# Threshold attention and maxout FFN on one core: another written order of the same work, with another list of masked score pieces

## The chip, the cores and the metric

The kernel runs on one core of one Trainium2 chip. The metric is device time in microseconds (us) from start to end of one execution. The kernel before took 447.18 us, the median of 3 runs (446.42 to 448.04).

## The reference

```
scores = scale * q @ k.T                     # batch 8, 8 heads, 576 x 576, head size 64
thresh = max(scores, axis=-1) - tau          # tau = 0.02
scores = where(scores >= thresh, scores, -1e9)
attn   = exp(scores - max(scores)); attn = attn / (sum(attn) + 1e-9)
x      = (attn @ v), heads side by side      # 4608 tokens x 512
h      = max(max(x @ w1, x @ w2), x @ w3)    # 768 wide
out    = h @ w_out                           # 4608 x 512
```

The softmax thus keeps only those scores of a row that lie within tau of the row's largest.

## The kernel before, in words

The attention of a batch is done in two quads of four heads, 16 quads in all. A quad is cut into nine chunks of 128 query rows, a chunk into two halves r of one head each; this gives 288 **score pieces** (a half chunk, 128 rows by 576 scores). A piece goes through this line, one letter for each step:

- `S` (`scores`, line 280, TensorE): the fp32 score matmuls into one of four PSUM slots; the digit behind the letter is the slot.
- `m` (`maximum`, line 312, VectorE, DVE): the row maximum, read out of the slot.
- `e` (`exponents`, line 324, ScalarE, ACT): the exponential, or the step that flattens the values below the threshold.
- `k` or `n` (`numerators`, line 332): the numerators and their sum, `k` on DVE, `n` on ACT.
- `r` (`reciprocals`, DVE), `p` (`normalized`, line 344, GpSimd, POOL) and `t` (`turned`, line 353, a transposing DMA issued by SP), the last for both halves together.

There are two ways through this line, and the string `MASKED` (line 24) chooses one for each piece, a bit each:

```
        if masked(c["g"], c["idx"], r):     # maximum: copies the scores out of PSUM
            vector.tensor_scalar(out=z_of(c, r), in0=c[r], scalar1=-1.0, ... accum_out=nm)
...
        if masked(...):                     # exponents: one ACT step, on the copy
            scalar.activation(out=zn, in_=zn, func=AF.Exp, bias=c["bias", r], scale=-1.0)
        else:                               # reads PSUM
            scalar.activation(out=zn, in_=c[r], func=AF.Prelu, ..., alpha=FLAT)
...
        if masked(...):                     # numerators, letter k
            vector.scalar_tensor_tensor(out=zn, in0=zn, scalar=thr, ... accum_out=acc)
        else:                               # letter n
            scalar.activation(out=zn, in_=zn, func=AF.Exp, scale=-1.0 / FLAT, accum_out=acc)
```

A **masked** piece costs DVE two passes (m, k) and ACT one (e), and its slot is free when m has read it. A **flat** piece costs DVE one pass (m) and ACT two (e, n), and its slot is free when e has read it.

The other letters: `T` transposes q or k of the next quad (evacuated by `a` on ACT for q and `c` on DVE for k, and copied across partitions by `q` on POOL); `O` multiplies numerators and values (evacuated by `x` on ACT or `w` on DVE); `F` is the first half of an FFN piece and `B` the second half of the oldest one begun, for the hidden layer (evacuated by `h` on ACT, `v` on DVE) and for the output projection (`u` on ACT, store `o` on SP). `l` and `g` are loads on SP, `y` and `z` casts on POOL. `S`, `T`, `O` and `F` each take one of the four slots.

The string `ORDER` (line 39) is the whole program after the prologue, one letter after the other; the loop at line 666 issues them. `_Ordered` (line 81) ties every instruction to the one before on the same engine, so each engine, SP included, works its letters off strictly in the written order, and across engines only the data and the buffers bind: a slot can be written again when its reader is done, `z` has four buffers for each half (`ZBUFS`), `P` six (`PBUFS`).

The last batch is split into two parts (`SPLIT`), so that the FFN of its first part fills TensorE while the attention of its second part ends.

Of the kernel before, what the change touches and what calls it, by code (L numbers as in the profile page):

```python
# [21 lines left out]
FLAT = 2.0 ** -100  # L22

MASKED = """
001100101001000000011101001010000001100010001000101000011000100000100000
000011111001100001001001001001000001011100101001000110001010010000010011
000010011101100001001100100001001010001100010111000001000100000110000101
001001001101100000110001000100100100001100100011100111010011010111110110
"""


# [5 lines left out]
PBUFS = 6  # L37

ORDER = """
lllS0llmlS1yelgS2ymylS3emgnlT0mleS1lakS2nlqermS3ylmeS0pmeS1kpS3elmS2nlzmelrmnT1pS0tcnperkT1pameS1zmteS3knpS0  # L40
rnmpemS2permeqS1mnqT3meqktepS0ncS2ntrpmS3npretprmeS1pmnS0tpmS3npmS1etpmeS0rT2mnplkeT1akgeS2qmgepmteS3rkpeknt
S0perrnmT2pncS3ptamepS1meqtrS2meyqnS3lmqeS0pmelpknT1lpS2nmeymeS3lrkepS0tcnT2rpnmS1tpnmaprrmS0eS2pmteS1pmT3ep
ctepmeT3O0ykntnyS2etrykpnO1wnprmaS0xptrS3meS2zmeS1mzgeS0mlnS3pmleS1pmelO2qmelpkteO0nrnklpS3nlwgxprrmS2leS0pm
eF3qtmT1eBqcF0eqkthBpnS2vS1nF3pmnF0pmBerBkepS2vhT1tnprmS0S3apmetS1zmeS2rmpeF3tmF0epBkepF1tnBvBznvS2ghS3rymnF
0gmS1eplBrkepF2tnmF3BnpvBnqvT1S0hprrcT2S3pamS1eymzF2emBeqgkF0etyS3nS1vpnmtF2pBmezBveS3prgnS0mtS1phrmT3epO2me
tzeF0wpnS1gcqS2nmBqnmO3zekepgS1xvlF2nS3mtnF0rrmpBeBlpveS1lphS2mntF3zmeBrpS0evS1lpnmF2lnpS3rmleBptmS1nzvS0nS3
mtpnS2rpeF1rmepmtepS0mBepmtekF3ektekT2uBarklpukS0uqlS2urS1mlnS3pmleO0pmlepmelO2wtnkS1xrS0tepmF2myF3eBkepT1tB
hcF0nqvT2T1laByrcynS3qvS2nlqmF1tnpF0meS3pBelmBlhrrF2kpelS1vnBlprF3mnlS0pveBtprmS1hS2pmeS3tpmeS0pmF2emF1eBkeT
3BvatF0nvqT2T3BkqlaS1nrcS3phmtS2npmF0epF1mteBqkBeqF3lnvS2lnBrvplS0hmtpS1F3meS2mteBrmepS0vnpO1rekpnO3mtnpweS2
yrrtxS1mF0yymT3epBcnS1pvS2nptF3meS0pmeBomT2hS1okeF0omF3ntBkaBervS1ponrF2vpemS0ptuS3mpeF2metknT1T3rknBparrceS  # L50
0puS3mqtuS1mpeS2mpeS3lmF0peomepS1ketqT3S2ncBqnmlqnmlO3ekluktO1urnwperrS0pxS3mptnS2mS1pempS3etmF0peF2meBlkBel
S1khoF3nrmlF0pnBtvpBerrvS2phlS1mnpS3tmF0peS2mpeBmeF3vF1eoBkntS0vnBS2rmhpS3mepS1mteyF2mF0eyBkteBnrvT3pF1aovT2
ynBplrcS3hplS0mnyF2lmF1elBykepBlnvT3tS0aS2vnO3rrmtpnmpeS1weptS2mS0prmO3eqtmeqF1eqlT0S2xqcBnlpmS3hlpS0meF2ymF
1elBknlF3vnBokBetS2hvS0nrrF3mpF1mpeBkBpetF2vnprS0uvnT3ptmS2aS1pmeS0trmF3epmnpkeS2tS0ermpBnmopnkS1uS2rurompS0
eF3ompelmpeS2lkpeS0lmS1elqBmelqmetkO2unktO0erwpurkpT1txT2cS3apF0nmtT1qS2ceBqmnS1yF3hmF2eyrBpeBvptnF0pS1vnBrm
tpS3hS2pmeS0mtS1eF3meF2meBkBeF0knF1vnBBrvhpS3nvT0pF2akyF1tnBmyS0velByrmlS3phS2rlempF1lmyeF0pklBepS3tnvS2nBrm
ptO1meprvepS2wnS3plmF0nF1rmepBlkeqS2lBhmtT3nyS0vnS2mqlO1emtpecT2xT0rS3pacF1eqmF2lnyBklqeT0BvlaS3khoS1qnmF0tF
2pmeBrBopnvS3teprvF0pnrmS1puS2meS3prmS0epF1tmepmepT2ktBeqncT3tuS0kaS2urqmS3tnpmS1nF0pmemteS3repS1mS2lepmBely
kteS3kuO1rumplnmlpO0ewterpT2xS1cqnoS3mpF0nF2metBkeBkF1hlF3nvBlnrrS0pvlnBpmS2lhS1ymleF0mtS3epBmepF2vF1etkBnS0
vnS3rmBnpS2rhmpF0emF1pteBkpBerF3vnS2ptvnT0pBramS1pthS0mepF3meqtT2rBecpS1nvylT0ynS2pmlS3amlS1eomS0elO2rmpeome  # L60
plO3ketnwT1F0nctF2xkBnBrvpS1hrF3pmS0qBemqS2onvF1yeF0mBopkeF3tyBnS2vqhBrlrnmpT1S0vaptS2empF1S3mpelBkeplF0vntS
2rumS1pnS0mtepF3rmepmetqS2kS0epBnmmteS1rkepS2lmuS0ulpmS1nlymT3yetF2cekeT3oBrknpamoS0npS3mnS1qtmuO0qurrmqelO2
wpelkpelS0xS3meptF2mS1peBemytF0hrkT3pBecF2nS1vpnS3rymtBpnmS0epS1vlnF3mF2etBmeBkhF0lkeF3nBrvpS1nrvBpnS2mptS0h
mpeS3meF2tmF1eBkeBlrvnT0plS3ravlpS2nlmqF0nlS1mqeBtrrmpF2eS3phBlmepS0tvepS1mS2npS3mepO0meknO1meownT3orxkT2pS0
tacF1nF2qrmeBtpS3evpBmS0tyhF1meT2yBcqoeF3rpkT2F0aptBnvBnS2pvS1hqtmF3nqT0meBrS1npvF2npmT3BactS1ervF3prmS0pueS
2ompF3ekqelmT1ntS0qcnBpmekteS2S1urrmpF0uompekS3eptS2nmS1pnmlO3ermtpekO2pnwS1ykxtyS3emS2BomeyrmepS1rukpS2uoF3
meF0opmnBtykBhpS1ervS2eptmO3pO0mxnS3txS2rmepF0empF1ekBtBevF3hkS2nS0mnBrmF1npF2vepBkBtS0hvO3emO2xkS1xerS3rpmF
2mpF0eF1kpteBnBvpF3BvtBrhkpF2S0vS1prmBptmF3eF0pveBtBhS1vS2mS3mF0F1mBkBF2vhF3keBeO0vnO1kF2kxeBwurS1rvpS0mpS2F
3mpetmpeS0eoF1mnketBknkBurrupoF2puF0hptF3uvF2pvF1hF0tvF3rvpF2hF1vopF0vF3thF2vF1vF0hoF3vF2ovF1hF0vF3vO2uoO1wF
0xF3F2hF1vF3vF2hF1vF3vF2hF1vF3vF2hF1vF3vF2hF1vF3vF2hF1vBvF3uuooBF2uuuooo  # L70
"""


# [633 lines left out]
```

## Time and profile before

| | |
|---|---|
| median of 3 runs | 447.18 us |
| profiled execution | 447.21 us |
| its span, first to last instruction | 445.4 us |
| TensorE matmul (PE) busy | 425.5 us, 96% |
| DVE busy | 395.1 us, 89% |
| ACT busy | 393.8 us, 88% |
| POOL busy | 314.9 us, 71% |
| mean granted TensorE clock | 0.985 |

The profiled execution has its own time, 447.21 us, of which 445.4 us are the span and 1.8 us lie around it. PE stands for TensorE's matmuls and PEld for its weight loads; all operations go through the helper `_Ordered`, so nearly all rows bear its line, L90, and are told apart by the tiles: `sc` is a slot of scores, `z` the values of a piece, `unused` the output of a flat piece's maximum, `tp` a transpose, `o` a product, `ph` a hidden piece, `po` an output piece.

### The profile page before, as it was taken

The numbers are of one execution on the slowest core, as the hardware profiler recorded it, in microseconds if no ns is written. First come the engines' busy times: TensorE is split into PE (matmuls) and PEld (weight loads), VectorE is DVE, ScalarE is ACT, GpSimd is POOL, SyncE is SP. The second block draws the span as 40 slices with busy tenths as digits, with TensorE's granted clock in tenths as the row PEclk, the third lists the DMA queues.
The fourth block names the chain that finished last, engine by engine and source line by source line (L and its number), as shares of the span: only waits on it lengthen the run. The fifth ranks groups of instructions, "written<-read, shape, count | busy, mean of one in ns | idle before, by whom it ended". The sixth has DMA issues, their size and how long they took to land.

```text
span 445.4 us, 14085 instructions
## 1 busy us (share of the span) xinstructions
PE 425.5 (96%) x5195; PEld 316.4 (71%) x5195; DVE 395.1 (89%) x1093; ACT 393.8 (88%) x801; POOL 314.9 (71%) x417
## 2 busy tenths in 40 slices
PE   7677799999999999999999999999999999999995
PEld 5455557767787767778687767867687778777772
DVE  4889999999999999989989998999999999989641
ACT  4999999999999999999998999999999999956422
POOL 3797999989686686686768884859767789562300
PEclk9967999999999999999999999999999999999999
DMA  7999999999999988999996999899998978872902
GB/s 235 344 163 216 251 169 241 227 245 230 222 250 195 244 165 177 252 191 253 187 175 158 238 206 167 207 249 203 208 208 192 249 121 172 149 122 34 217 13 107
DMA packets 212773, 87.44 MB, mean 196 GB/s; under 512 B 185824, under 2 KB 199648, under 8 KB 212704
## 3 DMA queue, kind: packets, MB, share of 16 engines
q1 hardware_dynamic: 212000, 85.69, 92.2%
q8 instruction: 41, 0.67, 0.6%
q10 hardware_dynamic: 704, 0.85, 0.6%
q14 instruction: 28, 0.23, 0.2%
HBM read 34.60 MB, written 9.44 MB: 99 GB/s over the span
## 4 chain that ended last, share of the span: by engine, by line
PE 82%; DVE 6%; ACT 5%; issue 3%; DMA 2%; POOL 1%; SPq 1%; DVEq 0%; POOLq 0%; ACTq 0%
PE ph L90 30%; PE sc L90 28%; PE po L90 11%; PE o L90 9%; ACT z L90 4%; PE tp L90 4%; DVE unused L90 2%; DVE z L90 2%; DMA km<-in_k_dram 1%; DMA qm<-in_q_dram 1%; POOL P L90 1%; SPq L90 1%; DVE hm L90 0%; DVE hT L90 0%; DVE kt L90 0%
## 5 line engine op out<-in xcount | busy, mean ns | idle before, releaser
L90 POOL TENSOR_SCALAR P<-z,rs 128x576 bf16<-128x576 f32 x288 | 229.5, 812 | 85.1 <-DVE rs L90 36.8
L90 PE MATMUL sc<-kt,qs 64*128 64x256 f32 (+2 forms) x640 | 180.5, 423 | 4.8 <-DVE z L90 1.7
L90 PE MATMUL sc<-kt,qt 64*128 64x320 f32 (+2 forms) x640 | 181.1, 434 | 4.1 <-ACT z L90 4.1
L90 PE MATMUL ph<-xt,w 64*128 64x288 bf16 (+2 forms) x2160 | 163.8, 283 | 0.3
L90 PEld LDWEIGHTS <-w 64*128 64x128 bf16 (+1 forms) x2160 | 124.8, 94 | 31.0 <-issue 5.1
L90 DVE TENSOR_SCALAR_CACHE_REDUCE unused<-sc 128x576 bf16<-128x576 f32 x183 | 133.3, 750 | 8.5 <-PE sc L90 7.5
L90 ACT ACTIVATE z<-sc,nm 128x576 f32<-128x576 f32 x183 | 131.2, 740 | 10.5 <-DVE unused L90 6.8
L90 ACT ACTIVATE z<-z 128x576 f32<-128x576 f32 x183 | 123.5, 681 | 0.1
L90 PEld LDWEIGHTS sc<-kt,qs 64*128 64x128 f32 (+1 forms) x640 | 94.3, 181 | 25.5 <-ACT z L90 7.0
L90 PEld LDWEIGHTS sc<-kt,qt 64*128 64x128 f32 (+1 forms) x640 | 94.5, 181 | 17.8 <-ACT z L90 9.2
L90 DVE SCALAR_TENSOR_TENSOR z<-z 128x576 f32<-128x576 f32 x105 | 85.2, 822 | 0.8 <-ACT z L90 0.8
L90 DVE TENSOR_SCALAR_CACHE_REDUCE z<-sc 128x576 f32<-128x576 f32 x105 | 77.7, 752 | 5.8 <-PE sc L90 3.5
L90 ACT ACTIVATE z<-z,nm 128x576 f32<-128x576 f32 x105 | 79.0, 773 | 3.5 <-DVE z L90 3.2
L90 POOL COPY qs<-qt 64x512 f32<-64x512 f32 (+1 forms) x63 | 44.6, 707 | 15.7 <-ACT qt L90 12.6
L90 PE MATMUL po<-wo,hT 64*128 64x512 bf16 (+1 forms) x480 | 54.0, 356 | 0.1
L90 ACT ACTIVATE hm<-ph 128x576 bf16<-128x576 f32 (+2 forms) x54 | 32.1, 594 | 18.5 <-PE ph L90 18.1
L90 DVE TENSOR_TENSOR hm<-ph,hm 128x576 bf16<-128x576 f32 (+2 forms) x54 | 37.0, 686 | 12.8 <-PE ph L90 11.6
L90 PEld LDWEIGHTS <-hT 64*128 64x128 bf16 (+1 forms) x480 | 29.6, 97 | 17.1 <-issue 2.9
L90 DVE TENSOR_TENSOR hT<-ph,hm 128x576 bf16<-128x576 f32 (+2 forms) x54 | 37.1, 688 | 3.3 <-PE ph L90 0.8
L90 PE MATMUL o<-ptq,vb 128*64 128x64 bf16 (+2 forms) x544 | 38.7, 282 | 0.0
L90 ACT ACTIVATION_READ_ACCUMULATOR z<-z 128x1 f32 x183 | 36.4, 199 | 0.0
L90 PEld LDWEIGHTS <-vb 128*64 128x64 bf16 x544 | 22.6, 111 | 15.1 <-issue 6.1
(33 smaller groups left out, 275.2 us busy)
## 6 DMA issues: line engine op xcount, KB each, us to landing
vm<-in_v_dram SPq DMA_DIRECT2D x32, 256.0 KB, 5.2
out_dram<-ob SPq DMA_DIRECT2D x31, 256.0 KB, 2.8
qm<-in_q_dram SPq DMA_DIRECT2D x15, 512.0 KB, 4.4
km<-in_k_dram SPq DMA_DIRECT2D x15, 512.0 KB, 5.1
stage<-in_moe_w_dram SPq DMA_DIRECT2D x9, 512.0 KB, 5.2
ptq<-P SPq DMA_TRANSPOSE x144, 3.9
stage<-in_moe_w_out_dram SPq DMA_DIRECT2D x3, 512.0 KB, 4.6
qm<-in_q_dram SPq DMA_DIRECT2D x16, 64.0 KB, 2.7
```

Of the source, the lines that this page charges most:

```text
L90: ins = fn(*a, **kw)
```

## The change

The strings `MASKED` and `ORDER` are replaced; no other line differs. Both orders have 2742 letters and the same number of every letter, but for k and n: 105 pieces were masked and 183 flat, and now 100 are masked and 188 flat. 31 of the 288 bits differ. Masked pieces by their place:

| pieces | before | after |
|---|---|---|
| 1 to 24 | 9 | 6 |
| 25 to 72 | 12 | 14 |
| 73 to 96 | 10 | 9 |
| 97 to 264 | 59 | 59 |
| 265 to 288 | 15 | 12 |

```
 MASKED = """
-001100101001000000011101001010000001100010001000101000011000100000100000
-000011111001100001001001001001000001011100101001000110001010010000010011
-000010011101100001001100100001001010001100010111000001000100000110000101
-001001001101100000110001000100100100001100100011100111010011010111110110
+010000101000100000011000101010000011000010001000101000011000100000100100
+000011110001100001001001001001000000111100101001000110001010010000010001
+010010011101000001001100100001001010001100010010110001000100000110000101
+001001011101100000110001000100100100001100100011100101011001100101001110
...
 ORDER = """
-lllS0llmlS1yelgS2ymylS3emgnlT0mleS1lakS2nlqermS3ylmeS0pmeS1kpS3elmS2nlzmelrmnT1pS0tcnperkT1pameS1zmteS3knpS0
-rnmpemS2permeqS1mnqT3meqktepS0ncS2ntrpmS3npretprmeS1pmnS0tpmS3npmS1etpmeS0rT2mnplkeT1akgeS2qmgepmteS3rkpeknt
-S0perrnmT2pncS3ptamepS1meqtrS2meyqnS3lmqeS0pmelpknT1lpS2nmeymeS3lrkepS0tcnT2rpnmS1tpnmaprrmS0eS2pmteS1pmT3ep
+lllgS0llmlS1yelS2nmlT3emS0keS1armpnS2pmeztS3emnS0qmelS1ymyeS3gymleS2mlS1eyyrT0nqcnpmT0npmetrkepS3nS2rlpnmzem
+tS3epS1emplakS2nlqS0erlrmqnS3lmpempeT1klpnT2tcerpmnS1S0gpnmleprmS1leptS3apmekS0qtemnT2qmeS1rkepT3cnS0tpnmS2n
+rrS1mpatpmnT3pmeS2tpemeS0qrklS2eqekS1gnptmnpmetymeS0rrncS2pmnpS3kepteS1rmnpS0mntprmeS3pmeT2tpS1empemtakS0nqO
...
-2mpF0eF1kpteBnBvpF3BvtBrhkpF2S0vS1prmBptmF3eF0pveBtBhS1vS2mS3mF0F1mBkBF2vhF3keBeO0vnO1kF2kxeBwurS1rvpS0mpS2F
-3mpetmpeS0eoF1mnketBknkBurrupoF2puF0hptF3uvF2pvF1hF0tvF3rvpF2hF1vopF0vF3thF2vF1vF0hoF3vF2ovF1hF0vF3vO2uoO1wF
-0xF3F2hF1vF3vF2hF1vF3vF2hF1vF3vF2hF1vF3vF2hF1vF3vF2hF1vBvF3uuooBF2uuuooo
+tBBevF0nF1vBkBhkS2nF3rvnpF0mBpS1rvptBrmS2phS3meptS0mepF2emF1tekBBevF3noF0vnoS2kF1orBmpBrhpBvF2pvO3pO0wS1xuS3
+emoS0mF2emtekF1nketBknnrrpBurpuptF3uF0phF2vF3ptvF0hpF2uvF3tvF1hF0vF2vF3ohF1voF0vF2ohF3voF1vF0hF2vF3vO1uoO0wF
+2xF3F1hF0vF3vF1hF0vF3vF1hF0vF3vF1hF0vF3vF1hF0vF3vF1hF0vBvF3uuoBF1ouuuooo
```

The first transposes of the second quad now stand behind three score pieces instead of four, and the first weight load ahead of the first piece. The first product stands behind 40 score pieces and the first FFN piece behind 51, in both orders. From the last score piece on, the two orders hold nearly the same letters, with other slots.

More of the change, by code (lines that the diff above doesn't have):

```diff
@@ L39 @@
 ORDER = """
-lllS0llmlS1yelgS2ymylS3emgnlT0mleS1lakS2nlqermS3ylmeS0pmeS1kpS3elmS2nlzmelrmnT1pS0tcnperkT1pameS1zmteS3knpS0
-rnmpemS2permeqS1mnqT3meqktepS0ncS2ntrpmS3npretprmeS1pmnS0tpmS3npmS1etpmeS0rT2mnplkeT1akgeS2qmgepmteS3rkpeknt
-S0perrnmT2pncS3ptamepS1meqtrS2meyqnS3lmqeS0pmelpknT1lpS2nmeymeS3lrkepS0tcnT2rpnmS1tpnmaprrmS0eS2pmteS1pmT3ep
-ctepmeT3O0ykntnyS2etrykpnO1wnprmaS0xptrS3meS2zmeS1mzgeS0mlnS3pmleS1pmelO2qmelpkteO0nrnklpS3nlwgxprrmS2leS0pm
-eF3qtmT1eBqcF0eqkthBpnS2vS1nF3pmnF0pmBerBkepS2vhT1tnprmS0S3apmetS1zmeS2rmpeF3tmF0epBkepF1tnBvBznvS2ghS3rymnF
@@ L45 @@
[L45 to L64, printed above, removed]
@@ L65 @@
-tacF1nF2qrmeBtpS3evpBmS0tyhF1meT2yBcqoeF3rpkT2F0aptBnvBnS2pvS1hqtmF3nqT0meBrS1npvF2npmT3BactS1ervF3prmS0pueS
-2ompF3ekqelmT1ntS0qcnBpmekteS2S1urrmpF0uompekS3eptS2nmS1pnmlO3ermtpekO2pnwS1ykxtyS3emS2BomeyrmepS1rukpS2uoF3
-meF0opmnBtykBhpS1ervS2eptmO3pO0mxnS3txS2rmepF0empF1ekBtBevF3hkS2nS0mnBrmF1npF2vepBkBtS0hvO3emO2xkS1xerS3rpmF
-2mpF0eF1kpteBnBvpF3BvtBrhkpF2S0vS1prmBptmF3eF0pveBtBhS1vS2mS3mF0F1mBkBF2vhF3keBeO0vnO1kF2kxeBwurS1rvpS0mpS2F
-3mpetmpeS0eoF1mnketBknkBurrupoF2puF0hptF3uvF2pvF1hF0tvF3rvpF2hF1vopF0vF3thF2vF1vF0hoF3vF2ovF1hF0vF3vO2uoO1wF
@@ L70 @@
-0xF3F2hF1vF3vF2hF1vF3vF2hF1vF3vF2hF1vF3vF2hF1vF3vF2hF1vBvF3uuooBF2uuuooo
+lllgS0llmlS1yelS2nmlT3emS0keS1armpnS2pmeztS3emnS0qmelS1ymyeS3gymleS2mlS1eyyrT0nqcnpmT0npmetrkepS3nS2rlpnmzem
+tS3epS1emplakS2nlqS0erlrmqnS3lmpempeT1klpnT2tcerpmnS1S0gpnmleprmS1leptS3apmekS0qtemnT2qmeS1rkepT3cnS0tpnmS2n
+rrS1mpatpmnT3pmeS2tpemeS0qrklS2eqekS1gnptmnpmetymeS0rrncS2pmnpS3kepteS1rmnpS0mntprmeS3pmeT2tpS1empemtakS0nqO
+2etrkpeO3mnprwnT1ptS2ecpnS0mztS1nmS2errmpxgmpeS3lezT0mlnS1kplaS3melO0pmngzelO2wlerklnpS0txS1rmpeS2mepS3mF1eq
@@ new lines @@
+mF0ntqBkeT3qBhrF2cnS1pvnS3mpgBemF0pevBlynyT1rkS2hlpemS0tpaS3rmepS1mtnF2pmS3ezrBemF1zevF0BekpS2tnvBnS3pmhF1tm
+qeF0kqnBtBrevF2pnS3vnptBmT1yhS0rrcnT3gS2pmaS1epmtF3erpmBekqS0teS2vnF1pmF3nmtyBepBrveS0pghS1mznS2mT3epO0gmetp
+rceS1yknqF3tnS2wBnpmS0nmpO1erzrvtemS3zxF2gmnF1pkeBpgBevS0lhS3prmlnF2pmleBprS1elvS0pnlmF3plnS2mtBzemS0nrS1vze
+tS2mepS3nF0pmeprmeS1pmBepmetkF2ekntkT3uS1akBnlrmpuS3ulpS1umlyS0errS2mlepO3mlepmelO1pwetkqS0xT3tnmF2qnF1cyBpe
+kBhtT3F0ravpT2nBrctS3qnvS1qnF2mlpF0meS3pBemlpBhlrkF1yeS2vnBlpmF3nytS0veBrprmS2hlS1ymeS3lpmeF0tpmS1epBemF2pvT
@@ new lines @@
+3eBkaF0tvnT1T3BcnS2tarkpS1hmnS3tF0mqeF2mqeBtBepvF1nqS3vlnBqrrmS0hpS2lmeF3plmS1elpBmeoS0pvnoO2keonkO3lntwrS1m
+xpS2rtmepF3mepT0BcepS1rvS0npF2mnyS3tmpeS1mBeyF0mtnF3khT1BaktS2evBnF1rvtpeS0rmpuS3mpeF1tkpemT2noT0BknlercptS3
+arrpuS2muS0ptmeS1pmeS2qmF3elmqnS0knplT2mBelpcetrS1kepS2urmO0ulpnmlpnO3owpekeqS0lS1xrtmqS2nmS3peF0mlepF1omBeo
+kBeS2tkhF3nrmF0ptBnvyBeyrrvS1phS2mnpS3mF0eptS1mepBmnF3ptvF2eBrkepS0nvBtS1pmhS3nmtS2emF1emF0teBkBevF3nlT2vT1a
+BrcplS0hrS2plmnF1lpmF3eBkoqeBvlnT0S2lpavS1tnmqO0nmqleqS3wtnS1rrmS2pemO0pempetkF3peT1BxcS2htrS0pmnS1prmF3eoF2
@@ new lines @@
+pmeBpnBtvyF1nS0veBtkS3hrF2mpnF1meBykpBeF0rvnptT3uvS2aprS0mnpS1tmF3eyrqmeS2kyeS0mnS1mepS2BepmtnpmS0erktpF1emu
+lkqS2uS0nlmS3eplrmBepmleS2pluO0mutekO1ektnwT3xrT2rpcS0aF1lpnmT3BpceS2thqS3mF0nqmF1elyBryleBpvlnF2poS3vnpBrmS
+0phtS1mepS2mS3eytF0meF1myeBkBetF2knF3rvBpBhvpS0nvF2tnF1mBnkT3oeS0vBlarrmS2phlS3mpelF1mpelF0kBpelS2rlvnBlpmnS
+3tpvO1ermnptS0wnpS2meF3qmF1eqBrkeS0tphBmnS2yvtS3eyT0mnO1mplecyT3xT2lrrT0pacS1oF3qmaoF2qekoBeBplS0vhtS1pmnF3p
+mF2etBrkepS0vnBS1pmnS3nrvpF0emtpS2umeS1mF0oekeT3mntBrcnpekT2tpS3arS1muptS2urmeS3qmF0elympelkS1nptS3nmS2pemBe
@@ new lines @@
+tqknS3uO1rmpumepO2wetkeT0xS1rcpS3nomF2pF0rmetqBkeBqF1hrlF3nyvlBnlS2vynBpmS0hS1pmeF2ptmS3eBpmeF0tvnF1kBeS2nvl
+S3nrlmBpS0lmhF2yempF1eBrktpBevF3npT0vS2ntBrraprmS1hpS0melyF3meT2BlepcS1ntpvT0nS2pmS3amlpS1elrS0mpelO2mpetmeq
+O3kelqnowT1F0xlrkpF2nlBcnS3lvqnBlrqmF1hS0lpeS2mlpBormF3eptF0veByykBptF1hvS2npBmnT0S3vaS2meF1qmS0teBrkepF3vno
+S2prumnS1ptmS3eF0pmemtnS2rkpeS3BmetpmekS1utS3urmpnT2mS0pntF1ceqmeS3okeT2BkelrarmpS0tukS2puS3nmO1pertmepmO0ek
+qtewS2xpS3lmnF1pmS0oeBkleF2rmhlT3pBcteS1qvF3npS0rmnlBpmelS2pvS1nlF0ymteF3mBekBeF2rkhpF1tnBvS0nprrvBnopS3mhS2
@@ new lines @@
+pmleS1pomF3epmF0teBkeBrtvT2npS1avS3ynytmF2pnS0meBlrrmpF3elS1phBlmepS2lveS0qmlS3nqS1mlepO2mtemnO0ketwnT1rxT3r
+pcS2aF0emqF1kBqeS3ovnBpmS2hF0ptmeT1pBncF3ntkF1eBvBntrrvpT2hS0pS3amF1ptmT2eBpceF3ytT0rvnS2kBnqF1amvS0pueS2rmp
+T1F3mpteceqS0nqS1mBnqmeykpS2eS0rumF1putmeykeS3pS2rnmS0ptmeO3pmnktO2ewnrkS0xpS3ermS2pmBeptrmepF0kuS2opuS3emF1
+nymBoBrhktpS3eS0vnO2mytO1pxmeS2prxS0meptF1empF3ekF2ytBeBvBhkS0nF1vnF3mBBevS2hkO0rO1mpxS3rxpeS0mpF2tmS1epF3me
+tBBevF0nF1vBkBhkS2nF3rvnpF0mBpS1rvptBrmS2phS3meptS0mepF2emF1tekBBevF3noF0vnoS2kF1orBmpBrhpBvF2pvO3pO0wS1xuS3
```

## The prediction

> **What bounds the kernel now.** The page's first part says little by itself: PE is busy for 96% of the span, DVE and ACT for 89% and 88%. So I read the stages next (busy time by stretch; columns: span of the stretch, then PE, PEld, DVE, ACT, POOL, with the granted TensorE clock, DMA share and GB/s last).
>
> ```profile
> 7.50:30.00 22.50, 15.19 (x126) 9.30 (x122) 19.72 (x57) 20.66 (x44) 18.77 (x24) 0.91 1.01 258
> 30.00:52.00 22.00, 17.17 (x128) 12.40 (x129) 19.90 (x60) 21.17 (x45) 19.04 (x26) 0.78 1.07 232
> 52.00:75.00 23.00, 21.59 (x260) 14.58 (x258) 22.36 (x62) 22.83 (x49) 21.99 (x28) 1.00 1.03 202
> 75.00:99.00 24.00, 23.86 (x308) 17.43 (x306) 22.73 (x59) 23.32 (x49) 23.28 (x29) 1.00 1.08 230
> 99.00:255.00 156.00, 155.66 (x2019) 117.88 (x2016) 147.76 (x410) 149.79 (x304) 116.51 (x157) 1.00 1.02 210
> 255.00:392.00 137.00, 137.00 (x1750) 104.25 (x1747) 128.76 (x362) 130.50 (x267) 100.69 (x135) 1.00 0.96 194
> ```
>
> Up to 75 us ACT is the full engine (21.17 of 22, 22.83 of 23) and PE has gaps; from 75 us on PE has none (292.9 of 293 from 99 to 392). The waits from 7 to 99 us (waiting engine and tile, releaser: us, times, longest) say the same:
>
> ```profile
> PEld sc L90 <- ACT z L90: 12.4, 17, 2.0
> ...
> PE sc L90 <- ACT z L90: 5.7, 6, 1.5
> ...
> ACT z L90 <- DVE unused L90: 2.9, 8, 0.7
> ```
>
> PE waits there for ACT to free score slots; ACT itself waits little. From 90 to 409 us the row PEld sc <- ACT z holds 3.9 us. So the kernel has **two regimes**: ACT sets the pace until some 67 us, then PE runs through to the end, the tail included. Hence end = (ACT work up to the slot that PE waits for last) + (ACT's idle time before it) + (all PE work behind it) + (small waits later).
>
> **The durations.** ACT and DVE work is taken from start to start, since a row's duration overlaps with the next one:
>
> ```profile
> 17.56 0.74 ACT L90 ACTIVATE z<-sc,nm 128x576 f32<-128x576 f32 x1 [0.33 <-DVE unused L90]
> 18.20 0.67 ACT L90 ACTIVATE z<-z 128x576 f32<-128x576 f32 x1
> 18.78 0.19 ACT L90 ACTIVATION_READ_ACCUMULATOR z<-z 128x1 f32 x1
> 18.87 0.67 ACT L90 ACTIVATE z<-z 128x576 f32<-128x576 f32 x1
> 19.44 0.19 ACT L90 ACTIVATION_READ_ACCUMULATOR z<-z 128x1 f32 x1
> 19.53 0.77 ACT L90 ACTIVATE z<-z,nm 128x576 f32<-128x576 f32 x1
> 20.24 0.60 ACT L90 ACTIVATE qt<-tp 128x512 f32<-128x512 f32 x1
> ```
>
> A flat e is 0.64 (17.56 to 18.20), an n 0.67 (18.20 to 18.87), a masked e 0.71 here and 0.69 in the mean. On DVE an m is 0.68 in both forms and a k 0.75 in the mean. So a piece that turns flat **adds 0.62 us to ACT** (0.64 + 0.67 - 0.69) **and takes 0.75 us from DVE**. Five net flips: ACT +3.1 us, DVE -3.75 us. PE's work is a set of pieces between neighbours, medians from start to start: a score piece 0.48 ahead of its other half and 0.53 to 0.54 ahead of other work; half a hidden piece 0.49 (a chain row has 32 ph matmuls in 1.96), a product 1.3 (40 in 2.59), half an output piece 1.3, transposes 0.25 to 0.34.
>
> **The change, part by part.**
>
> *ACT in front.* For each PE letter that takes a slot I add up ACT's work in the written order up to the read that frees the slot, and take off PE's work in the order ahead of that letter; call it ACT's lead. Where it is largest, PE waits for ACT last. The largest lead in each dozen of pieces, before and after:
>
> - pieces 37 to 48: 19.6 and 20.7 us
> - 49 to 60: 20.7 and 21.5
> - 61 to 72: 20.7 and 21.7
> - 97 to 108: 18.7 and 20.0
> - 193 to 204: 10.4 and 12.2
> - 265 to 276: 5.6 and 6.2
>
> Both rise until some 60 pieces and fall from there: past the peak PE is slower than ACT, and the slots come free in time. Peak before: the score piece after 57 others, 64.9 of ACT less 44.2 of PE. The trace has this piece at 76.1 us, that is 64.9 + 11.2; ACT's first e is at 8.78, so ACT was idle or handing over for 2.4 us by then. From there PE has 361.8 us of work up to the start of its last letter: 76.1 + 361.8 = 437.9, and the trace has 440.1, so 2.2 us of waits come later. The peak after is at the 67th piece, 80.3 of ACT less 58.6 of PE. **This costs +1.0 us.** The flips in the first 24 pieces (-3 masked) are the reason, only partly undone in 25 to 72 (+2). What is added after 73 lies beside PE's work: the lead there is under the peak, by 1.7 us at piece 100 and by 9.5 at piece 200.
>
> *DVE in front.* The same sum for DVE peaks at 15.5 us before and 14.1 after, 5 to 8 us under ACT's, so DVE frees no slot last. Its 3.75 us go at no gain of their own, but ACT waits 2.9 us for DVE up to 99 us, and a DVE with 1.6 us less work by piece 15 can take some of that away. Also, the first two waits of ACT (0.69 and 0.46, at 8.78 and 9.98) change: after has the first n between the first two e's, which fills the second. Bounds: 0 (new waits of the same size) to -2.4 (all idle gone). I take **-1.0**, the middle, as the nearest row (0.46, and half of the rest) gives about that.
>
> *PE's work.* The same letters, but other neighbours: before has 83 score pieces directly ahead of their other half, after 77, 0.05 us each, +0.3; products and output pieces meet other letters. All neighbours summed by the medians of before: 406.0 against 406.8 us. Some medians rest on one to three cases, so I take **+0.4**, with 0 and +0.8 as bounds.
>
> *Slots later on.* From the 73rd to the 270th piece slots are taken again with less than 2.0 us (masked) or 2.5 us (others) of PE work between in fewer places, 113 after against 123 before, and those are the places where PE waits. By the waits of before it would save up to 1.0 us; but all waits behind the peak come to 2.2 us, some of them in the tail, which is unchanged. I take **0**, with -1.0 as bound.
>
> *The start.* The first transposes of the second quad stand behind three pieces instead of four, but they wait for a load anyway (PE idles 1.46 us, until 11.55). The fourth piece now waits behind them, and comes 2.7 us later. By 12.1 ACT has done the same work in both (two flat e, one n, one masked e), so this costs nothing, or up to 0.7 where the fourth piece's m comes too late for its e. SP has the first weight load one place ahead of one k load; the transposes of k stand 12 pieces in, beyond 16 us, so this is hidden.
>
> *The tail.* In before, the last products start at 423.1 us, 4.1 after POOL's last normalisation; after has 1.3 us more PE work between the last score piece and them. Three masked pieces fewer there make ACT's end later by 1.9 us, where ACT is busy for 12.9 of 21 us. Hidden; if it were not, 0.5 us.
>
> **Sum:** 447.21 + 1.0 - 1.0 + 0.4 + 0 = **447.6 us**. The profiled run stands 0.03 above the median, so the same holds for the median.
>
> **Rivals.** Differences under 0.3% (1.3 us) can't be told from no change by a measurement of this kernel.
>
> 1. *Forecast, within 0.3%:* ACT's deeper work and its lost idle time cancel. Chance 0.42, 446 to 448.5.
> 2. *Faster:* a DVE with less to do feeds ACT without gaps in front (-2.4 instead of -1.0), the slots turn over with less waiting (-1.0) and PE's neighbours cost nothing (0). 447.2 + 1.0 - 2.4 - 1.0 = 444.8; with two thirds of it, 445.4. For it: DVE is 88% to 97% busy up to 99 us, so it does make ACT wait. Against it: ACT idles for only 1.0 us in 30 to 75 us. Chance 0.30.
> 3. *Slower, by ACT in front:* ACT is 99% busy from 52 to 75 us, so each new wait of ACT there, and each added n, goes one for one into the end. It decides once ACT's idle time before the peak is not smaller than the 2.4 us of now. Nothing regained, and as much idle time added as 30 to 52 us shows now (21.17 of 22, 0.8): 447.2 + 1.0 + 0.4 + 0.8 = 449.4. Chance 0.21.
> 4. *Slower, by the clock:* the clock was 0.91 and 0.78 in the two stretches in which PE was busy for 68% and 78%, and 1.00 from 52 us on, where it is 94%; the lost shares, 2.0 and 4.8 us, are two stretches of 6.8 us at half clock (0.5 x 13.6). One more such stretch after 52 us would cost up to 3.4 us: 451.0. Chance 0.07, since PE's work ahead of the 54th piece is the same in both orders to 0.3 us. [...]
>
> That the new order does nothing is no case of its own: it would be inside the first.
>
> **How the numbers follow.** Likeliest is the first case, 447.6. Low end: the second case in full, 444.8. High end: the third with a part of the fourth, 450.0; beyond it lies most of the fourth. Faster by over 0.3%: 0.30; slower: 0.21 + 0.07 = 0.28; within: 0.42.
>
> **What would show it.** Right: ACT over 99% busy between 30 and 75 us, the 67th score piece between 90.7 and 91.7 us (91.1 before), PE without gaps from there. The step on ACT's idle time is wrong if ACT's waits for DVE before 75 us are unchanged; the step on PE's work if the time from the 90th score piece to the end (317 us) moves by over 1 us. The forecast as a whole is wrong if the time is lost or won behind 100 us, for there I count nothing.

## The result and the profile after

The kernel after took **448.07 us** (median of 22 runs, 446.65 to 450.99), the kernel before 446.80 us in 22 runs of the same sessions. The ratio is **1.0027, interval 1.0014 to 1.0040**: 0.6 to 1.8 us slower, within the 0.3% that the forecast called no change, though the interval reaches to 0.4%. The profiled execution of after took 448.48 us, its span is 446.6 us (before: 447.21 and 445.4).

The same stretches as before, of the kernel after (span of the stretch, then PE, PEld, DVE, ACT, POOL, granted clock, DMA share, GB/s):

```profile
7.50:30.00 22.50, 16.26 (x146) 9.92 (x144) 18.87 (x54) 21.56 (x45) 18.86 (x26) 0.92 0.97 252
30.00:52.00 22.00, 17.38 (x124) 10.07 (x121) 20.04 (x62) 21.44 (x47) 20.16 (x26) 0.85 1.15 234
52.00:75.00 23.00, 21.36 (x257) 13.16 (x258) 20.64 (x60) 22.79 (x49) 20.47 (x27) 1.00 0.96 217
75.00:99.00 24.00, 23.69 (x303) 16.84 (x303) 23.17 (x62) 23.46 (x51) 22.68 (x29) 1.00 1.13 231
99.00:255.00 156.00, 155.05 (x2012) 118.48 (x2010) 147.36 (x403) 149.33 (x301) 115.07 (x156) 1.00 1.01 208
255.00:392.00 137.00, 136.99 (x1751) 103.07 (x1751) 130.10 (x359) 130.77 (x266) 101.22 (x134) 1.00 0.99 186
```

Read it against the table of before. In front ACT is fuller (43.00 of 44.5 us up to 52 us, before 41.83) and DVE has 1.7 us less in 52 to 75; that is what the flips do. The row in which PE lost most is 99 to 255 us: 155.05 busy of 156, before 155.66. The waits from 7 to 99 us (waiting engine and tile, releaser: us, times, longest):

```profile
PEld sc L90 <- ACT z L90: 14.1, 22, 2.3
...
PE sc L90 <- ACT z L90: 6.1, 9, 1.8
PEld sc L90 <- DVE z L90: 4.2, 9, 1.2
...
ACT z L90 <- DVE unused L90: 1.4, 3, 0.6
```

ACT's waits for DVE fell from 2.9 to 1.4 us; PE's waits for ACT rose from 18.1 to 20.2 us. From 90 to 409 us the row PEld sc <- ACT z holds 5.3 us where before had 3.9.

**Where the time went.** The same score piece can be compared by the start of its first matmul (us; the middle column is the difference that PE's own work in the order ahead of it, at the medians of before, accounts for):

| score piece | before | after less before | by PE's own work |
|---|---|---|---|
| 1 | 7.13 | +0.63 | 0 |
| 36 | 48.54 | -0.47 | -0.07 |
| 67 | 91.09 | -0.14 | -0.05 |
| 90 | 123.89 | -0.21 | -0.03 |
| 134 | 183.55 | -0.43 | +0.10 |
| 158 | 216.18 | +0.63 | +0.18 |
| 180 | 251.12 | +1.27 | +0.51 |
| 252 | 351.77 | +0.40 | +0.55 |
| 270 | 376.72 | +1.12 | +1.21 |
| last PE letter | 440.13 | +1.17 | +0.82 |

Up to the 134th piece nothing is lost. Behind it 1.60 us are: by these sums 0.72 by PE's neighbours and 0.88 by waits. Some of the medians rest on few cases, but PE's idle time in the records says much the same: behind the 134th piece it is 0.07 us in before and 1.03 in after. Of the first 0.63, a wait of PE for a load of q makes 0.50 (until 7.22 us; before's execution has none there). The kernels below have their first piece at 7.3 to 8.6 us with the old start and at 7.2 to 8.5 with the new, so this belongs to the execution and not to the order.

One trace is one execution, and executions of one front differ. At the 134th piece the kernels below that share before's front stand 0.16, 0.57 and 1.01 us behind before (back_after, dve_back, act_back); with the new front, after stands at -0.43, front_after at -1.31 and k_later at +0.39. So the new front is some 0.9 us quicker in the mean, with a spread of 1 to 1.7 us within each. From there to the end the traces part more clearly: with before's order and nothing added there they lose 0 to 0.7 us against before (act_front, unmask_front, dve_front), with after's 1.0 to 1.6 (after, remask_front, remask_defer).

The largest of the waits, in time order on DVE, POOL and PE (start, duration, operation, idle time before and its releaser):

```profile
210.39 1.58 DVE L90 SCALAR_TENSOR_TENSOR z<-z 128x576 f32<-128x576 f32 x1
...
211.91 0.75 DVE L90 TENSOR_SCALAR_CACHE_REDUCE z<-sc 128x576 f32<-128x576 f32 x1
```

```profile
210.33 1.04 POOL L90 CAST vb<-vm 128x1024 bf16<-128x1024 f32 x1
211.35 2.69 POOL L90 TENSOR_SCALAR P<-z,rs 128x576 bf16<-128x576 f32 x3
```

```profile
212.72 0.48 PE L90 MATMUL sc<-kt,qs 64*128 64x256 f32 x1 [0.60 <-DVE z L90]
```

A k that mostly takes 0.75 us takes 1.58 here, because POOL's cast of v began 0.06 us ahead of it; the masked m behind it frees its slot 0.8 us later, and PE, whose written order has no other work first, waits (0.7 to 0.8 us by the matmul starts, the row shows 0.60). The other waits of PE over 0.2 us behind the 120th piece are 0.28, 0.21 and 0.32 us in after, 0.30 and 0.21 in before.

### The profile page after: what moved, and what is told of

Its sections match the earlier page's. It is cut to its first block, busy times and chain, and to the rows that moved or that the text cites. A ratio compares the mean times of both kernels' runs of the same rounds, so it can differ in the third digit from the quotient of the medians.

```text
span 446.6 us, 14090 instructions
## 1 busy us (share of the span) xinstructions
PE 426.3 (95%) x5195; PEld 314.5 (70%) x5195; DVE 393.8 (88%) x1083; ACT 397.3 (89%) x811; POOL 312.6 (70%) x417
## 4 chain that ended last, share of the span: by engine, by line
PE 81%; ACT 5%; POOL 3%; DMA 3%; DVE 3%; issue 3%; SPq 1%; DVEq 0%; POOLq 0%; ACTq 0%
PE ph L90 29%; PE sc L90 29%; PE po L90 10%; PE o L90 9%; ACT z L90 5%; PE tp L90 3%; DMA vm<-in_v_dram 3%; POOL P L90 2%; DVE unused L90 1%; DVE z L90 1%; SPq L90 1%; POOL qs L90 1%; DVE hm L90 1%; DMA out_dram<-ob 1%; DVE hT L90 0%
## 5 line engine op out<-in xcount | busy, mean ns | idle before, releaser
L90 POOL TENSOR_SCALAR P<-z,rs 128x576 bf16<-128x576 f32 x288 | 227.4, 804 | 90.2 <-DVE rs L90 46.3
L90 PE MATMUL ph<-xt,w 64*128 64x288 bf16 (+2 forms) x2160 | 165.6, 283 | 0.5 <-DVE hT L90 0.2
L90 PEld LDWEIGHTS <-w 64*128 64x128 bf16 (+1 forms) x2160 | 127.2, 94 | 31.1 <-issue 6.3
L90 DVE TENSOR_SCALAR_CACHE_REDUCE unused<-sc 128x576 bf16<-128x576 f32 x188 | 136.8, 750 | 7.8 <-PE sc L90 6.8
L90 ACT ACTIVATE z<-sc,nm 128x576 f32<-128x576 f32 x188 | 135.3, 743 | 6.9 <-DVE unused L90 5.5
L90 ACT ACTIVATE z<-z 128x576 f32<-128x576 f32 x188 | 127.2, 682 | 0.1
L90 PEld LDWEIGHTS sc<-kt,qt 64*128 64x128 f32 (+1 forms) x640 | 92.7, 179 | 20.1 <-ACT z L90 9.9
L90 DVE TENSOR_SCALAR_CACHE_REDUCE z<-sc 128x576 f32<-128x576 f32 x100 | 74.2, 751 | 9.7 <-PE sc L90 5.8
L90 ACT ACTIVATE z<-z,nm 128x576 f32<-128x576 f32 x100 | 75.5, 772 | 3.1 <-DVE z L90 2.6
L90 POOL COPY qs<-qt 64x512 f32<-64x512 f32 (+1 forms) x63 | 47.8, 759 | 11.7 <-ACT qt L90 8.5
```

The lines of the kernel that those rows point to most:

```text
L90: ins = fn(*a, **kw)
```

## The experiments

Two theories. **ACT alone**, the prediction's: in front ACT sets the pace, DVE has 5 us and more in hand (the prediction adds up nothing for POOL), and behind it PE runs through. **Joint**: in front ACT, DVE and POOL are bound together by their in-order queues and the z buffers, and any of them can set the end.

**Half of the change each.** `front_after` has the new order and mask up to the 134th piece and the old ones behind, `back_after` the reverse.

> The new order and mask list up to the 134th score piece, the old ones from there on (103 pieces masked). Theory A, from the two profiles: the new front is about 1.0 us quicker by piece 137, counted from the first score piece, and the loss of 1.2 us as a whole arises behind it. Then this kernel takes 1.0 us less than before, ratio 0.998. Theory B, the forecast's own: ACT's deeper work in front (+1.0 us) is the loss, and the back is equal. Then it takes 1.0 to 1.3 us more than before, ratio 1.003.

> The old order and mask list up to the 134th score piece, the new ones from there on (102 pieces masked). Theory A: the new back loses some 1.6 us (1.0 of it between pieces 137 and 161, the rest behind 245), so 1.6 us more than before, ratio 1.0035. Theory B: no change, ratio 1.000.

Measured: front_after 447.28 us, ratio 1.0005 (0.9986 to 1.0024); back_after 449.01 us, 1.0043 (1.0024 to 1.0061). In the traces front_after's last PE letter is 0.35 us earlier than before's, and back_after's difference grows from +0.16 at the 134th piece to +1.81 at the end. The wait at the 155th piece is there in back_after too, at 213.85 us, the same to 0.01 us. So the loss is in the back, and it comes with the written order, not with what the front hands over. The halves do not add up closely to the whole, 0.05% and 0.43% against 0.27%, within their intervals, and part of that is the seam, where the two orders meet: both traces have a wait of PE for DVE's z behind the 135th piece (until 183.95 and 185.43 us) that costs 0.6 us by the piece starts and that neither before nor after has. Without it, by an estimate, front_after would stand 0.9 us ahead of before and back_after 1.2 us behind it.

**Is the wait at the 155th piece the cause by itself?** `k_later` is after with that k one step later, behind the masked m that the slot waited for:

```
-...yrqmeS2kyeS0mnS1mep...
+...yrqmeS2yeS0mknS1mep...
```

> The new kernel with one letter moved: the k of piece 149 stands behind the m of piece 152 instead of ahead of it. In the new kernel's trace this k starts at 210.39 us, 0.06 us behind a cast of v on POOL (1.04 us), takes 1.58 us instead of 0.75, and the m behind it frees a slot that PE waits for (0.81 us). Theory C, that this one collision is half of the loss behind piece 134: the stall goes and the time falls by 0.7 us, to about 1.0010 of before. Rival, that PE only shows there what it would lose elsewhere: no change, 1.0027.

Measured: 448.31 us, 1.0031 (1.0015 to 1.0047), as slow as after. The wait is gone, and another one stands two pieces on:

```profile
212.48 1.01 DVE L90 SCALAR_TENSOR_TENSOR z<-z 128x576 f32<-128x576 f32 x1
```

```profile
216.99 0.18 PEld L90 LDWEIGHTS sc<-kt,qs 64*128 64x128 f32 x1 [0.81 <-ACT z L90]
```

The moved k now meets a P of POOL (1.01 us), and PE waits 0.48 us for ACT at the 157th piece. From the 154th to the 158th piece PE falls back 0.71 us against before, where after falls back 0.80. So this one collision is not the cause by itself. That DVE and ACT have too little room in this stretch, so that a mended wait comes up again near by, is how I read it; no run shows it apart.

**Added work on ACT or on DVE.** Before with five passes put in that nobody reads, on ACT (copies 128x448, 0.47 us each) or on DVE (128x448, planned as 0.55 us), behind the e or the m of pieces 25 to 49 (front) or 191 to 231 (back):

```
+        elif what == "d":
+            scalar.activation(out=one_junk(), in_=Ls[made[-1]["g"]]["kt"][:, 0, 0:448], func=AF.Copy)
+        elif what == "D":
+            vector.scalar_tensor_tensor(out=one_junk(), in0=src, scalar=thr, in1=src,
...
```

> The kernel before with five more copies on ACT (128x448 values, about 0.5 us each, 2.4 us in all, output unused), one behind each e of pieces 25, 31, 37, 43 and 49. If ACT sets the pace in front: 1.5 to 2.4 us more, nearly all of it. If PE or DVE sets it: 0 to 0.7.

> The same five copies behind the e of pieces 191, 201, 211, 221 and 231. If PE sets the pace there, as the lead sums say (ACT's lead 9 us under its peak): 0 to 0.5 us more. If ACT, 96% busy there, still counts: 1.5 to 2.4 us more.

> The kernel before with five more passes on DVE (scalar_tensor_tensor on 128x448 values, about 0.55 us each, 2.8 us in all, output unused), behind the m of pieces 25, 31, 37, 43 and 49. If DVE stands 5 us under ACT in front, as the lead sums say: 0 to 0.7 us more. If DVE binds there as well: 1.5 us or more.

> The same five passes behind the m of pieces 191, 201, 211, 221 and 231, where DVE's lead is 10 to 13 us under the peak. By the lead sums: 0 to 0.5 us more. If a DVE pass there delays the next m past the slot's turn, as the collision at 210 us did: 1 to 2 us more.

| run | added, in the trace | median | ratio, interval | trace: later by, at its place |
|---|---|---|---|---|
| act_front | 2.3 us | 448.45 | 1.0032 (1.0016 to 1.0049) | 2.3 |
| act_back | 2.3 us | 447.68 | 1.0017 (0.9997 to 1.0037) | 0.9 |
| dve_front | 4.6 us | 451.41 | 1.0101 (1.0083 to 1.0118) | 2.2 at piece 90, 2.8 at the end |
| dve_back | 3.1 us | 448.86 | 1.0044 (1.0028 to 1.0060) | 1.6 |

The DVE passes took more than planned. They read the same SBUF tile twice, and in front four of the five began while POOL was working; from start to start they held DVE for 0.54, 0.77, 1.04, 1.17 and 1.05 us. Operations of POOL that began during them were longer too (P 0.99 to 1.17 us). The last section shows the rule. So these runs load DVE and POOL together, not DVE alone.

ACT in front comes out at the end for a good part, as the prediction had it: 1.4 us (0.7 to 2.2) by the times, all of the 2.3 in the trace, whose execution (449.60 us) is the second longest of its twelve. But so does the work on DVE: the time rose by 4.5 us (3.7 to 5.3), and the profiled execution, with 450.10 us the shortest of its five, by 2.8, where 0 to 0.7 was expected of a DVE with 5 us in hand. **ACT alone falls here.** In the back DVE's passes are not free either: 2.0 us (1.2 to 2.7) of 3.1 come out at the end. For ACT there the trace shows 0.9 us at its place, but the times can't be told from no loss.

**The flips in front taken back.** `remask_front` is after with pieces 12, 22 and 24 masked again, n to k in place, 103 masked.

```
-010000101000100000011000101010000011000010001000101000011000100000100100
+010000101001100000011101101010000011000010001000101000011000100000100100
```

> The new kernel with pieces 12, 22 and 24 masked again, their n turned into k at the same place (103 masked). ACT has 1.9 us less and DVE 2.25 us more to do ahead of the peak. If ACT alone sets the pace in front: 1.0 to 1.9 us less than the new kernel, ratio 0.9985 to 1.0005 of before. If ACT, DVE and POOL bind there by turns (the new front alone gained and lost nothing): within 0.5 us of the new kernel, 1.0015 to 1.004.

Measured: **451.85 us, 1.0122 (1.0103 to 1.0142)**, slower than after instead of faster, by 3.8 us by the medians and 4.2 by the ratios. By the durations of the prediction ACT has 1.9 us less to do, and its idle time between 9.5 and 52 us rose from 0.7 to 5.8. What it waited for shows in the waits of ACT in this stretch, after first, then remask_front:

```profile
ACT z L90 <- DVE unused L90: 0.9, 2, 0.6
ACT z L90 <- DVE z L90: 0.2, 1, 0.2
```

```profile
ACT z L90 <- DVE unused L90: 3.7, 4, 1.3
ACT z L90 <- DVE z L90: 1.6, 4, 0.7
```

And the chain of waits of remask_front (start, duration, engine and tile), where after has POOL until 31 us, DVE and PE until 36 and then ACT:

```profile
20.55 1.47 POOL P L90 x2
22.04 0.77 DVE z L90 x2
22.81 0.09 DVE rs L90
22.90 0.08 issue
22.98 1.18 POOL P L90
24.18 0.78 DVE z L90 x2
25.01 1.45 PE sc L90 x4
26.48 0.77 DVE unused L90 x2
27.25 1.76 DVE z L90 x4
29.01 0.20 DVE rs L90 x2
29.21 0.72 DVE unused L90 x3
...
46.83 1.16 DVE z L90 x3
47.99 0.69 DVE unused L90 x2
48.76 0.63 ACT z L90
```

The same chain of after, its longest steps behind 26 us:

```profile
26.90 2.82 POOL P L90 x4
...
34.90 1.02 DVE unused L90 x3
...
36.35 2.74 ACT z L90 x7
...
41.42 3.17 ACT z L90 x6
...
47.91 3.40 ACT z L90 x7
```

From 26.5 to 48.7 us every long step but a few matmuls is DVE's, which is busy for 21.51 of 23 us between 26 and 49 (in after 21.04); ACT has 18.86 there, in after 22.31. The first lines show the second tie: POOL P, then DVE z, then POOL P again. A masked m writes a z buffer and has to wait until POOL has read out of it the chunk that stands four before.

**Which of the two ties costs it?** Two runs give remask_front what each would need. `remask_z5` has five z buffers (and four P buffers, for the room); `before_z5`, its control, is before with that change alone. `remask_defer` has the three k written one to three steps later, so that they hold up DVE's queue less.

```
-ZBUFS = 4
-PBUFS = 6
+ZBUFS = 5
+PBUFS = 4
```

> The kernel after with pieces 12, 22 and 24 masked again (the run remask_front, 451.85 us), and five z buffers in place of four, paid for with two P buffers (six to four). The change of buffers alone is the run before_z5; the two are read together. Theory D: in front a masked piece's m on VectorE writes into the z buffer of the chunk four before it, and waits for GpSimd's P that still reads that buffer (trace of remask_front: m at 22.04, 24.18 and 35.81 us behind POOL P); with a fifth buffer these waits go, and the time falls by 2 to 3.5 us, to 448.3 to 449.9. Rival K: it is VectorE's own work and its written order (three more k of 0.75 us each, which wait for e at the head of VectorE's queue); the time stays within 1 us of 451.8.

> The kernel before with five z buffers in place of four and four P buffers in place of six; order and mask untouched. Theory D (z buffers tie VectorE's m to GpSimd's P in front): 0 to 1 us faster, 445.8 to 446.8, since the trace of before has only small waits of that kind. Rival: four P buffers are too few, P on GpSimd waits for TensorE's matmul to give one back, and the time rises by 1 to 5 us.

> The kernel remask_front (pieces 12, 22 and 24 masked again, 451.85 us) with the k of these three pieces written one to three steps later in the order, so that k waits less for its e at the head of VectorE's queue; same pieces, same buffers. Rival K (VectorE's queue is held by a k that waits for ScalarE's e): the time falls by 1 to 2.5 us, to 449.3 to 450.9. Theory D (the z buffer that m waits for): no change, within 0.7 us of 451.8, since the m's still wait for POOL P.

Measured: before_z5 456.11 us, 1.0206 (1.0182 to 1.0229); remask_z5 457.82 us, 1.0260 (1.0243 to 1.0276); remask_defer 451.69 us, 1.0115 (1.0101 to 1.0130). Four P buffers are too few, and that hides most of the answer in the times; these are the waits of POOL in before_z5 between 52 and 92 us, of which before has nothing:

```profile
POOL P L90 <- DMA ptq<-P: 5.1, 2, 4.0
```

But up to the 36th piece this has not begun yet, and there the traces can be compared: before_z5 stands at 47.12 us (before 48.54), remask_z5 at 50.88. The three masked pieces cost 3.8 us there with five z buffers, and 4.1 with four (remask_front 52.19, after 48.08); before_z5 has the order of before, which has this piece 0.47 later than after, so that with one order it would be some 4.2 against 4.1. So **a fifth z buffer does not give the time back**. It does not clear the tie either: in the waits between 9.5 and 52 us DVE z <- POOL P holds 1.7 us in remask_z5, 1.9 in remask_front. With the order of before these waits are gone, where before had 0.7 us, and piece 36 comes 1.4 us earlier; with one trace each that is a hint that the z buffers cost time in both fronts, and no more. The place of the k in the queue is not the reason: remask_defer is as slow as remask_front.

What makes three k cost some 4 us stays open. Their own 2.25 us do not cover it, and up to 30 us DVE is not full: from 9.5 to 30 us it is busy for 16.08 of 20.5 us, in after for 18.11. Over half of the loss against after is there by piece 24 (2.3 us of 4.1, in remask_defer 2.9). What the traces show there is that DVE and POOL wait for each other: POOL P <- DVE rs holds 5.7 us between 9.5 and 52 us (after 2.5), DVE z <- POOL P 1.9 (after 1.1). No run has five z buffers and six P buffers together.

**The other way round.** `unmask_front` is before with pieces 3, 4 and 29 flat, k to n in place.

> The kernel before with pieces 3, 4 and 29 turned flat (three k's of VectorE become three n's of ScalarE in place; 102 masked). If ScalarE alone paces the front, its lead over VectorE grows by three n's less nothing: 1.0 to 1.9 us slower, 447.8 to 448.7. If VectorE and GpSimd bind the front as much as ScalarE (as remask_front and dve_front suggest), the three k of 0.75 us that leave VectorE give back as much as the n's take: between 1 us faster and 0.5 us slower, 445.8 to 447.3.

Measured: 448.46 us, 1.0040 (1.0024 to 1.0056). The profiled execution took 447.26 us, near the shortest of its twelve, and its trace has no loss: ACT is busy for 1.45 us more in 9.5 to 75 us, which were idle in before, the 90th piece starts 0.18 us later than in before, the last letter 0.05. The median thus speaks for ACT's work coming out at the end, this one trace for its being filled into gaps. Since traces of one front differ by 1 us and more, the trace does not outweigh the median, but the two are not reconciled.

## Why the prediction came out as it did

The time fell where the first case had put it, 447.6 forecast and 448.07 measured. That is in part luck: the front, forecast at 0, came out some 0.9 us quicker in the mean of the traces, the back, forecast at +0.4, 1.0 to 1.6 us slower, and the two errors partly cancel.

- **ACT in front, +1.0, and idle time of ACT regained, -1.0: borne out in part, not measured apart.** ACT's idle time between 9.5 and 75 us fell from 2.15 to 0.93 us, and its waits for DVE there from 2.6 to 0.9. The 67th piece starts at 90.95 (forecast 90.7 to 91.7, before 91.09), and the half with only the front of the change is at 1.0005, its seam included. But k_later, with the same front, has this piece at 91.3 and front_after at 90.2, so that the hit is within the spread of one front. ACT's share in 30 to 75 us is 98.3%, not the 99% that was to be seen.
- **DVE in front, "5 to 8 us under ACT's, so DVE frees no slot last": wrong.** dve_front and remask_front lost 4.5 and 3.8 us by work that such a reserve would have hidden (how much of it by way of POOL, these runs do not separate). The sum of DVE's work up to a slot counts DVE as if it could run ahead; up to 75 us its work on z alone waits in after for PE's scores (1.2 us), for POOL (1.1) and for ACT (0.3), so the reserve can't be saved up. More work on either engine comes out at the end (act_front, dve_front), and a flip in front pays 0.62 us on the one for 0.75 us on the other. The forecast let DVE's relief count only through ACT's short waits, and POOL not at all, on which after's chain runs until 31 us.
- **PE's neighbours, +0.4 with 0.8 as bound: the term was mis-sized.** The sums of 405.99 and 406.81 us that it halved were right: 0.85 us between the 90th piece and the end. The time from there to the end went from 316.24 to 317.61 us, +1.37, over the 1 us that was to show this step wrong: 0.85 of it by the full sum of the neighbours, the rest by waits. PE's rows were also read too full: 155.66 and 137.00 us from 99 to 392 are 292.66 of 293, not 292.9.
- **Slots later on, 0 with -1.0 as bound: wrong sign.** By the forecast's count fewer slots are taken again soon, yet the waits from the 90th piece on are 0.5 us longer, 0.9 behind the 134th. The count asked what lies between on PE; the wait at the 155th piece came from DVE and POOL, which it left out. The forecast as a whole was to be wrong if time were lost behind 100 us, and by that sign it was: all of the +1.2 us is there, and only its size kept it within the case.
- **Start and tail, 0: nearly right.** From the last score piece to the last letter after takes 31.79 us, before 30.19; by the same medians 1.40 of the 1.60 is PE work that was moved there (it is counted above), 0.2 is waiting.
- **The clock: no stretch after 52 us, which is what the rival needed.** The rows give 0.92, 0.85, then 1.00. Ahead of 52 us the trace of after does have three stretches at half clock, of 3.41 us each (from 23.1, 30.0 and 47.0 us), where before has two of 6.83 (from 26.1 and 39.7), so that the lost shares are 5.1 us for 6.8. All five follow a stretch of 3.41 us in which PE was busy for 1.6 to 2.0 us.
- **The other rivals.** "Slower, by ACT in front" did not come, as ACT's idle time fell; "faster" did not come, since the back lost more than the front gained. (Two thirds of the gain in "faster" give 445.6 us, not 445.4; nothing else rests on it.)

## What to carry to other kernels

Work added up along one engine's order gives its lead only if it never waits for the others; with in-order queues and few buffers, test each engine near 90% busy with a few passes that nobody reads before calling one the bound, and measure in the trace what these passes took and whom they held up. Moving a piece between two engines that both bind need not change the time by the piece's own size: here -1.9 us on ACT and +2.25 us on DVE cost 3.8 us. Take more than one trace of a kernel before reading a difference of 1 us out of a stretch with waits. In a stage where one engine runs through, sum its neighbours' times in full, and look at the order of the others for operations that meet on a shared port, but expect that mending one such place moves the wait on.

## What the runs showed of the hardware

A k (DVE, both inputs the same z in SBUF) that starts while POOL works on SBUF is held until POOL is nearly done. In after a k that meets no running POOL operation takes 0.73 to 0.76 us, in 52 cases. In 29 cases POOL had begun before the k and had 0.18 us or more left (P, a copy of q or a cast), and the k was longer by that rest less 0.13 to 0.14 us in each of them:

| POOL's rest when k starts | k longer by |
|---|---|
| 0.20 | 0.06 |
| 0.35 | 0.21 |
| 0.54 | 0.41 |
| 0.70 | 0.56 |
| 0.98 | 0.84 |

In three more cases the two began within 0.02 us of each other, POOL first by the record, and there POOL's operation was the one held: the k took 0.75 to 0.78 us, P and the copy 1.31 to 1.35. An m, which reads PSUM, is not held: 157 of them in after began with more than 0.3 us of a POOL operation left and took 0.73 to 0.76 us. The added passes of dve_front and dve_back, DVE operations with two SBUF inputs as well, were longer by POOL's rest less 0.14 to 0.15 us in the seven cases with a rest over 0.18.

The Trainium skill, "SBUF — State Buffer", section "Who interferes with whom", says that a DVE instruction with two SBUF inputs contends with a GpSimd instruction that reads SBUF, and that whoever comes second is blocked until the first is done. The trace agrees, but for the last 0.13 us or so, and in both directions: P takes 0.745 us by itself, and of the 288 P in after 37 took over 1 us. Of these 35 began while a k was running and were longer by the rest of that k less 0.13 us (the P behind the k of 210.39 us, for one, begins at 211.35 and takes 1.24); the other two are of the three cases above. Behind 183 us this adds 3.0 us to the k's of before (62 of them) and 5.4 us to those of after (59), so DVE lost there most of what five fewer k gave it.
